# Batch 0 of an attention and feed-forward kernel by head halves, with a new order of all instructions

## The chip, the core and the metric

The kernel runs on one core of a Trainium2 chip. A core has TensorE (PE, with its weight loads listed as PEld), VectorE (DVE), ScalarE (ACT), GpSimd (POOL) and SyncE (SP), each with its own queue of instructions that it works through in order, and 16 DMA engines that move data between the chip's main memory and the core's. DMAs are issued by SP, ACT or POOL. The metric is the device time of one execution in microseconds (us), the median of three runs.

## The reference, cut to what matters

```python
# q, k, v: (8 batches, 8 heads, 576 tokens, 64), w_in: (512, 2048), w_out: (2048, 512), float32
theta = pi / 2 * arange(576) / 576
def phi(x):                                  # 64 -> 128 features
    r = maximum(x, 0)
    return concatenate([r * cos(theta), r * sin(theta)], axis=-1)
kv  = einsum('bhsf,bhsd->bhfd', phi(k), v)   # per batch and head, 128 x 64
z   = sum(phi(k), axis=tokens)
num = einsum('bhsf,bhfd->bhsd', phi(q), kv)
den = einsum('bhsf,bhf->bhs', phi(q), z) + 1e-6
x   = (num / den) as (8 * 576 tokens, 512)
h   = x @ w_in
out = (h * cos(h)) @ w_out                   # (4608, 512) float32
```

The kernel computes in 16-bit floats with 32-bit accumulation.

## The kernel before, in words

**Tiling.** Each batch has 576 tokens, treated as four tiles of 128 tokens and a rest of 64. The rests of the eight batches form a ninth chunk of 512 tokens. `raw` holds the loaded q, k, v of one batch in 32 bits (tiles `qm`, `km`, `vm`). `prep` (L336) applies the relu and the cosine or sine factor to one token tile and writes 16 bits into `KQ` (L346 on ACT, L347 on DVE). `cast_v` (L351) casts v into `V1` (L360 ACT, L361 DVE, L362 POOL), beside a column of ones that yields z. `q_pe` (L396) transposes q on PE (L402) and copies it out of PSUM (L406 ACT, L408 DVE). `kv` (L365) is the key-value product over five token tiles (L373), copied into `kvz` (L385, L387, L390). `num` (L419) multiplies q with kvz (L435) and normalises on DVE: add 1e-6 (L451), reciprocal (L453), multiply (L455). `x_pe` (L468) transposes the result on PE (L475) and ACT copies it into `xT` (L479). From batch 2 on, many of these transposes are done by DMA instead (L412, L485).

**Layers.** `layer1` for batches 0 and 1 (L513 to L538) makes 16 groups of eight matmuls of 256 columns each (L529): four quarters of w_in, two halves of the 512 tokens (two token tiles each), two groups per quarter and half. A group ends in a bank of PSUM (`M1`, three of them), from which ACT takes the cosine (L502) and DVE the product (L504) into `gT`. `layer2_plain(0)` (L773) has eight groups of eight matmuls of 512 columns (L786): four token tiles for the first half of w_out (ACT copies the result, L794), then four for the second half (DVE adds, L797). Later batches use sums of operands to save matmuls (L596 to L720, L809, L822 to L928; their matmuls are L561, L667 and L861).

**The order.** `Plan` (L138) collects steps, each with the tiles it reads and writes. The order in which all steps are emitted, and the engine of each step that can run on more than one, come from two tables written out in the file, `STARTS` (L18) and `ENGS` (L118): steps are sorted by their entry in `STARTS`. The waits follow from the tiles. Every engine then works through its own queue in that order.

**Start.** `first_attention` (L988) clears the fifth token tile of k and v, runs 28 filler matmuls on constants (`warm`, L945), and loads q, k and v of batch 0 through SP, v in two head halves of four heads each. `weights` (L948) issues w_in in four quarters from POOL, with a conversion to 16 bits on the way (L956), behind a small POOL cast that reads k (L950), and the first half of w_out (L970) behind a small copy that reads w_in's first quarter (L960). After the q transposes come 17 more filler matmuls, k and v, both halves of `kv`, and then tile by tile `num`, filler (4, 3 and 2 matmuls) and `x_pe`.

**Second batch.** `second_attention` (L1015) loads k, q, v of batch 1, v in head halves, behind four small POOL casts (`hold_raw`, L973 to L977) that read the third quarter of w_in, the last one issued. The second half of w_out is issued (L970) behind a small POOL cast that reads q of batch 1 (`part_of_w_out`, L979 to L986). PE order around it: four groups of `layer2_plain(0)` among the rest of layer 1 of batch 0 and the transposes and products of batch 1; then the group of token tile 0 with w_out's second half; then two x transposes of batch 1 and layer 1 of batch 1.

Of the kernel before, what the change touches and what calls it, by code (L numbers as in the profile page):

```python
# [16 lines left out]

STARTS = (  # L18
# [166 lines left out]
def kernel(  # L185
# [12 lines left out]
    P = 128  # L198
# [816 lines left out]
    def second_attention():  # L1015
        T = start[1] - 30
        for nm in ORDER1:
# [4 lines left out]
            if nm == ORDER1[HOLDW]:  # L1022
                part_of_w_out(nm, 1)
# [103 lines left out]
```

## Time and profile before

| what | value |
|---|---|
| time, median of 3 runs | 281.58 us (281.47 to 283.69) |
| span of the profiled execution, first to last instruction | 279.7 us |
| PE busy | 272.6 us (97%) |
| PE weight loads busy | 215.5 us (77%) |
| DVE busy | 236.9 us (85%) |
| ACT busy | 210.2 us (75%) |
| POOL busy | 82.9 us (30%) |
| clock granted to TensorE | 1.00 in all stretches |
| data moved by DMA | 58.03 MB, mean 207 GB/s |
| last matmul ends | 275.0 us |

The profile comes from one execution; its own time is given only as this span, and the median of the runs is 1.9 us above it. All times in views of the trace count from the start of the span. Busy time of PE includes the modelled ends of pipelined matmuls, so a short wait between matmuls can hide in it. In the share lines "x" is the number of instructions. In lists of groups, `out<-in` names the tiles; the arrow in brackets at the end tells how long the engine stood idle before an instruction and what ended that.

### The profile page before, as it was taken

Reading aid. Unit: us, or ns where it says so; the run is one execution under the profiler, and the core shown is the slowest. Engines: PE = TensorE matmul, PEld = TensorE weight load, DVE = VectorE, ACT = ScalarE, POOL = GpSimd, SP = SyncE. Lnnn points to the kernel's source line nnn. Section 1 sums busy time; section 2 is a strip of 40 time slices with the busy share of each in tenths; the row PEclk is TensorE's granted clock in tenths of the full one; section 3 lists DMA queues with packets and bytes.
Section 4 is the critical chain, followed back from the end, with each engine's and each line's share of the span. In section 5 each row is a group of like instructions: output and inputs, shape, how many; then the busy total and the mean of one; then the engine's idle time right before and its main releaser. Section 6 shows DMA issues by size and latency. Waiting matters only on the chain.

```text
span 279.7 us, 6825 instructions
## 1 busy us (share of the span) xinstructions
PE 272.6 (97%) x2698; PEld 215.5 (77%) x2698; DVE 236.9 (85%) x442; ACT 210.2 (75%) x363; POOL 82.9 (30%) x102
## 2 busy tenths in 40 slices
PE   8999999999999999999999999999999999999993
PEld 2567857787966677769777878789988888888882
DVE  1767698989999999999999998989989879873952
ACT  2756699879998897788989988995758686776330
POOL 1430020030501201520340045132534372399210
PEclk9999999999999999999999999999999999999999
DMA  6999989999999999989999998549756495698125
GB/s 207 312 202 206 340 239 241 361 301 174 335 261 271 258 249 246 234 268 259 255 258 246 242 229 284 98 115 141 163 75 139 110 156 105 152 143 123 75 77 150
DMA packets 80223, 58.03 MB, mean 207 GB/s; under 512 B 43200, under 2 KB 77248, under 8 KB 80192
## 3 DMA queue, kind: packets, MB, share of 16 engines
q1 hardware_dynamic: 68960, 39.99, 59.4%
q0 software_dynamic: 10496, 17.04, 30.1%
q10 hardware_dynamic: 736, 0.57, 0.7%
q8 instruction: 21, 0.34, 0.5%
q14 instruction: 10, 0.08, 0.1%
HBM read 36.75 MB, written 11.80 MB: 174 GB/s over the span
## 4 chain that ended last, share of the span: by engine, by line
PE 92%; ACT 3%; DVE 2%; issue 1%; POOL 0%; ACTq 0%; POOLq 0%
PE M L861 34%; PE M L667 14%; PE M L561 11%; PE M L529 9%; PE TR L667 6%; PE ATT L945 5%; PE ATT L435 3%; PE M L786 3%; PE ATT L373 3%; PE TR L561 2%; ACT KQ L346 2%; DVE x L455 1%; PE M L402 1%; PE M L373 0%; PE TR L475 0%
## 5 line engine op out<-in xcount | busy, mean ns | idle before, releaser
L861 PEld LDWEIGHTS <-gT 128*128 128x128 f16 x560 | 53.9, 98 | 8.3
L861 PE MATMUL M<-w_out_sb,gT 128*128 128x256 f16 x448 | 57.1, 273 | 0.0
L504 DVE TENSOR_TENSOR gT<-M,ch 128x512 f16<-128x512 f32 x73 | 48.5, 685 | 5.9 <-ACT ch L502 5.7
L502 ACT ACTIVATE ch<-M 128x512 f32<-128x512 f32 x75 | 43.4, 596 | 12.0 <-PE M L529 5.4
L346 ACT ACTIVATE KQ<-km,CS 128x512 f16<-128x512 f32 x57 | 38.5, 717 | 1.4 <-DMA km<-in_k_dram 1.3
L872 ACT ACTIVATE ost<-M 128x512 f32<-128x512 f32 x41 | 24.3, 596 | 17.9 <-PE M L861 13.0
L346 ACT ACTIVATE KQ<-qm,CS 128x512 f16<-128x512 f32 x46 | 31.5, 720 | 4.1 <-DMA qm<-in_q_dram 4.1
L561 PE MATMUL M<-xT,w_in_sb 128*128 128x512 f16 x136 | 33.8, 379 | 0.0
L861 PE MATMUL M<-T,S 128*128 128x256 f16 x256 | 32.4, 273 | 0.0
L667 PEld LDWEIGHTS <-w_in_sb 128*128 128x128 f16 x288 | 27.3, 98 | 4.8 <-issue 0.3
L362 POOL CAST V<-vm 128x1024 f16<-128x1024 f32 (+1 forms) x18 | 15.9, 907 | 50.8 <-DVE den L451 20.7
L529 PE MATMUL M<-xT,w_in_sb 128*128 128x256 f16 x256 | 30.3, 273 | 0.3 <-DVE gT L504 0.3
L861 PEld LDWEIGHTS <-S 128*128 128x128 f16 x256 | 24.8, 98 | 4.1 <-DVE S L837 0.2
L529 PEld LDWEIGHTS <-w_in_sb 128*128 128x128 f16 x256 | 24.4, 98 | 3.9 <-issue 0.5
L679 DVE TENSOR_TENSOR Z<-M,Z 128x512 f32<-128x512 f32 x31 | 21.1, 687 | 4.3 <-PE M L667 3.1
L561 PEld LDWEIGHTS <-w_in_sb 128*128 128x128 f16 x160 | 14.9, 98 | 12.2
L504 POOL TENSOR_TENSOR gT<-Z,ch 128x512 f16<-128x512 f32 x5 | 6.3, 1268 | 56.6 <-ACT ch L502 20.0
L455 DVE TENSOR_TENSOR x<-ATT,rec 128x512 f16<-128x512 f32 x32 | 22.1, 691 | 1.1
L435 PEld LDWEIGHTS <-qT 128*128 128x128 f16 (+1 forms) x320 | 14.8, 101 | 5.6 <-issue 3.5
L690 ACT ACTIVATE ch<-Z 128x1024 f32<-128x1024 f32 x12 | 12.7, 1057 | 6.9 <-DVE Z L679 4.8
L675 ACT ACTIVATE Z<-M 128x512 f32<-128x512 f32 x26 | 15.1, 596 | 3.4 <-PE M L667 2.4
L435 PE MATMUL ATT<-kvz,qT 128*128 128x65 f16 (+1 forms) x288 | 16.0, 195 | 0.8 <-DVE x L455 0.5
(150 smaller groups left out, 519.3 us busy)
## 6 DMA issues: line engine op xcount, KB each, us to landing
out_dram<-ost POOLq DMA_DIRECT2D x38, 256.0 KB, 4.3
qm<-in_q_dram SPq DMA_DIRECT2D x8, 640.0 KB, 6.7
km<-in_k_dram SPq DMA_DIRECT2D x8, 640.0 KB, 7.1
qm<-in_q_dram SPq DMA_DIRECT2D x8, 512.0 KB, 6.0
km<-in_k_dram SPq DMA_DIRECT2D x8, 512.0 KB, 6.0
vm<-in_v_dram SPq DMA_DIRECT2D x6, 640.0 KB, 5.7
vm<-in_v_dram SPq DMA_DIRECT2D x6, 512.0 KB, 4.6
w_in_sb<-in_moe_w_in_dram POOLq DMA_DIRECT2D x4, 512.0 KB, 8.8
```

The source lines that it names most:

```text
L346: fn = {"ACT": lambda: nc.scalar.activation(out=out_, in_=in_, func=AF.Relu, scale=sc), "DVE": lambda: nc.vector.tensor_scalar(out=out_, i ...
L362: "POOL": lambda: nc.gpsimd.tensor_copy(out=out_, in_=in_)}
L435: nc.tensor.matmul(bank[hb][ps, hh * D1:(hh + 1) * D1], lhsT=x[:, h, :], rhs=z[:, h, :], start=True, stop=True)
L455: nc.vector.tensor_tensor(out=split(x16[n][:, hs, :], k), in0=A[:, :, :, 0:D], in1=split(rec[n][:, hs], k).unsqueeze(3).broadcast_to((P, k ...
L502: act(0.5, due, lambda: nc.scalar.activation(out=ch[c], in_=bank, func=AF.Sin, bias=math.pi / 2.0, scale=1.0), [key], [("ch", c)])
L504: mul(due, 0.61, lambda q: q.tensor_tensor(out=dst, in0=bank if len(dst.shape) == 2 else bank.rearrange("p (j s) -> p j s", j=dst.shape[1] ...
L529: nc.tensor.matmul(M1[m][:, jj * 2 * P:(jj + 1) * 2 * P], lhsT=w_in_sb[:, cc, j * P:(j + 1) * P], rhs=X[:, cc, ts], start=(cc == 0), stop= ...
L561: nc.tensor.matmul(M, lhsT=w_in_sb[:, cc, j * P:(j + 1) * P], rhs=X[:, cc, :], start=(cc == 0), stop=(cc == NCT - 1))
L667: nc.tensor.matmul(bank[0][:, j * TH:(j + 1) * TH], lhsT=a(cc, j), rhs=b[:, cc, :], start=(first and j == 0 and cc == 0), stop=(last and j ...
L679: dve(0.61, due + 0.3, lambda: nc.vector.tensor_tensor(out=dst, in0=bank[0], in1=dst, op=ALU.add), [bank[1], key], [key])
L861: nc.tensor.matmul(bank[0][:, tt * MH:(tt + 1) * MH], lhsT=a[:, j, tt * P:(tt + 1) * P], rhs=b[:, j, :], start=(first and (apart or tt == ...
L872: act(0.5, due, lambda: nc.scalar.activation(out=dst, in_=view(bank), func=AF.Copy), [bank[1]], dk)
```

## The change: what it does

It puts batch 0 on a path of its own, `first_attention_halves`. q stays as it was (relu steps and transposes of whole tiles). k is prepared per head half (four heads, 256 columns per step), v is cast per head half with two token tiles in one instruction, and `kv_half`, `num_pair` and `x_pair` work on one head half: `num_pair` fills two banks with two token tiles and normalises both tiles of the half in one set of three DVE instructions; `x_pair` transposes both tiles into one bank and one copy takes them to `xT`. Filler is 20 matmuls at the start, 12 around the first `kv_half`, and two per `num_pair`. Layer 1 of batches 0 and 1 goes through its groups in another sequence of quarters and token halves. In batch 1, v casts also take two token tiles at once, and steps can go to either engine.

On POOL, a further small cast (through the tile `HP`) stands between q of batch 1 and the cast that releases w_out's second half. The new code can also split w_in, with its second half behind the v casts (`WS2`), but this option is `None` here: the four quarters are issued together behind k, in the same order as before. `RAW1=2` and `WO2=1` name the same w_in quarter and the same tensor q as before. `STARTS` and `ENGS` are new for the whole program (1376 steps for 1363). Options not shown here (`F16`, `MODE`, `H1`, `DA`, `SQ`, `L2F` and others) are off and leave the steps as they were.

```diff
+OPT = dict(WS2=None, W2F=2, HH='kv', LD=[['q', 3], ['k', 3], ['v', 0], ['v', 1]], XB=[['B3'], ['B3', 'M1']],
+           W0=5, W1=6, WF=[[2, 2], [2, 2]], HOLD=['k', 0], P0=1, RAW1=2, WO2=1, ...)
...
-    den = [sb(f"den{n}", [P, H], F32) for n in range(NX)]
-    rec = [sb(f"rec{n}", [P, H], F32) for n in range(NX)]
-    x16 = [sb(f"x16_{n}", [P, H, D]) for n in range(NX)]
+    DEN, REC = [sb(n, [P, NX, H], F32) for n in ("den", "rec")]
+    den, rec = [[x[:, n] for n in range(NX)] for x in (DEN, REC)]
+    XN = sb("XN", [P, NX, H, D])
+    x16 = [XN[:, n] for n in range(NX)]
...
-            for quarter in range(4):
-                for hf in range(2):
+            for quarter, hf in ([(q_ + i, hf) for q_ in (0, 2) for hf in range(2) for i in range(2)] if OPT["HH"] else
+                                [(q_, hf) for q_ in range(4) for hf in range(2)]):
...
     def part_of_w_out(nm, n):
...
+        if OPT["W2F"]:
+            src, rd = raw[nm][0:2, 0, 0, 0:1], [((nm, 0), 0)]
+            for i in range(OPT["W2F"] - 1):
+                pl.add("POOL", 0.2, 0.3, 0, lambda i=i, src=src: nc.gpsimd.tensor_copy(
+                    out=HP[:, 2 + i:3 + i], in_=src), rd, [("hop", 2 + i)])
+                src, rd = HP[:, 2 + i:3 + i], [("hop", 2 + i)]
+            pl.add("POOL", 0.2, 0.3, 0, lambda src=src: nc.gpsimd.tensor_copy(
+                out=w_out_sb[0:2, n * JH:(n + 1) * JH, 0].rearrange("p (g j) -> p g j", g=2)[:, :, 0],
+                in_=src.broadcast_to((2, 2))), rd, [("w_out", g) for g in (2 * n, 2 * n + 1)])
+        else:
+            pl.add("POOL", 0.2, 0.3, 0, hold, hk(nm, [0], [0]), [("w_out", g) for g in (2 * n, 2 * n + 1)])
         w_out_load(2 * n, 2 * n + 2)
...
+    def kv_half(hb, bank, key, due, b=0):
+        hs = range(H)[HALVES[hb]]
...
+                for t in range(NT + 1):
+                    nc.tensor.matmul(
+                        bank[:, hh * D1:(hh + 1) * D1], lhsT=kp[:, t, h].rearrange("p g d -> p (g d)"),
+                        rhs=V1[:, t, h, :], start=(t == 0), stop=(t == NT))
...
+        copy_by_either(Z[:, hb], bank[:, 0:HB * D1], due, 0.4, 0.38, [key], [("kvz", b, hb)])
...
+    def num_pair(i, hb, due, b=0):
+        hs = HALVES[hb]
+        for t in (2 * i, 2 * i + 1):
+            bank, key = ATT[:, t % 2, :], ("ATT", t % 2)
...
+                for hh in range(HB):
+                    nc.tensor.matmul(bank[:, hh * D1:(hh + 1) * D1], lhsT=qT[t][:, hb * HB + hh, :],
+                                     rhs=kvz[b][:, hb * HB + hh, :], start=True, stop=True)
...
+        def norm():
+            nc.vector.tensor_scalar_add(out=denp[:, n], in0=A[:, :, :, D], scalar1=1e-6)
+            nc.vector.reciprocal(out=recp[:, n], in_=denp[:, n])
+            nc.vector.tensor_tensor(out=XF[:, hb, 2 * i:2 * i + 2], in0=A[:, :, :, 0:D],
+                                    in1=recp[:, n].unsqueeze(3).broadcast_to((P, 2, HB, D)), op=ALU.mult)
...
+    def half_tiles(hb, due):
...
+        for nm in OPT["HH"]:
+            if nm == "k":
+                for t in range(NT + 1):
+                    for g in range(2):
+                        prep(0, "k", t, g, "", due, hs)
+            elif nm == "v":
+                for t, nt in ((0, 2), (2, 2), (4, 1)):
+                    cast_v(0, t, ("DVE", "ACT", "POOL"), due, hs, nt=nt)
+                kv_half(hb, *BANKS2[hb], due)
...
+        if hb == 0:
+            for i in range(OPT["W1"]):
+                warm(2, 0.4314, ATT[:, 1, :], [("TR", 0)] if i == 0 else [], [("ATT", 1)])
+        if OPT["P0"]:
+            for i in range(NT // 2):
+                num_pair(i, hb, due + 2 * i)
+                n = OPT["WF"][hb][i]
+                if n:
+                    warm(n, 0.2157 * n, M1[1], [("ATT", 1)], [("M1", 1)])
+                x_pair(i, hb, *pick[kb_[i % len(kb_)]], due + 2 * i)
...
+    def first_attention_halves():
+        for i, nm in enumerate("kv"):
+            dve(0.53, i - 9, lambda nm=nm: nc.vector.memset(raw[nm][:, :, NT, :], 0.0), [],
+                hk(nm, ts=[NT]))
+        for i in range(OPT["W0"]):
+            warm(4, 1.293)
+        for nm, x in OPT["LD"]:
+            load(0, nm, 0, HALVES if x == 2 else (slice(0, H),) if x == 3 else (HALVES[x],))
...
+        for hb in range(2):
+            half_tiles(hb, 4 + 4 * hb)
...
-    first_attention()
+    (first_attention_halves if OPT["HH"] else first_attention)()
     layer1(0)
     second_attention()
```

More of the change, by code (lines that the diff above doesn't have):

```diff
@@ L282 @@
     ORDER0, ORDER1, HOLDW, W_FIRST = "qkv", "kqv", 1, None
-    GATE1 = (w_in_sb[0:2, 0, Dff // 2 + 1:Dff // 2 + 2], [("w_in", 2)])
+    R1 = OPT["RAW1"]
+    GATE1 = ((w_in_sb[0:2, 0, R1 * Dff // 4 + 1:R1 * Dff // 4 + 2], [("w_in", R1)]) if R1 < 4 else
+             (w_out_sb[0:2, (R1 - 4) * NJT // 4, 1:2], [("w_out", R1 - 4)]))
+    HOLDW, W_FIRST = OPT["WO2"], OPT["WFI"]
     src = {"k": k, "v": v, "q": q}
@@ L344, in prep @@
         f = len(heads) / H
-        cost = {"DVE": 0.09 + 0.33 * f, "ACT": 0.12 + 0.5 * f}
+        cost = {"DVE": 0.09 + FD * f, "ACT": 0.12 + 0.5 * f}
         fn = {"ACT": lambda: nc.scalar.activation(out=out_, in_=in_, func=AF.Relu, scale=sc),
@@ L362, in cast_v @@
               "POOL": lambda: nc.gpsimd.tensor_copy(out=out_, in_=in_)}
-        either(due, {e: cost[e] for e in ([eng] if eng else VCAST)}, fn, rd, wr)
+        either(due, {e: cost[e] for e in ([eng] if isinstance(eng, str) else eng)}, fn, rd, wr)
+    full = {}
     def kv(b, due, pair=None):
@@ L398, in q_pe @@
         ps = bank.bitcast(F16).rearrange("p (h s) -> p h s", h=H)
+        more = [("qTh", t % NT, hb) for hb in range(2)] if b <= 1 and OPT["HH"] else []
         def mm():
@@ L458, in norm, with norm2 @@
                     op=ALU.mult)
-        dve(1.05 if pair is None else 1.15, due, norm, keys, [("x16", n)])
+        if OPT["DA"] and pair is None and b >= 2:
+            A, (hs, k, ks) = N[0], cut[0]
+            act(0.22, due, lambda: nc.scalar.activation(
+                out=split(den[n][:, hs], k), in_=A[:, :, :, D], func=AF.Identity, bias=EPS, scale=1.0),
+                keys, [("den", n)])
+            def norm2():
+                nc.vector.reciprocal(out=rec[n], in_=den[n])
+                nc.vector.tensor_tensor(
+                    out=split(x16[n][:, hs, :], k), in0=A[:, :, :, 0:D],
+                    in1=split(rec[n][:, hs], k).unsqueeze(3).broadcast_to((P, k, HB, D)), op=ALU.mult)
+            dve(0.87, due, norm2, keys + [("den", n)], [("x16", n)])
+            return n
+        dve(1.05 if pair is None else 1.15, due, norm, keys, [("x16", n)]
+            + ([("x16h", n, hb) for hb in range(2)] if b == 1 and OPT["HH"] else []))
         return n
@@ L476, in mm @@
                                  is_transpose=True)
+        full[key] = False
         pe(NCT, MMT, due, mm, [("x16", n), "ID", *after], [key])
@@ L577 @@
     LATE = min(c for c, nf in FAST1.items() if nf > 2)
-    assert all(FAST1[c] == NJT // 4 for c in range(LATE, NC))
     def flat(t, dt=F16):
@@ L946, in warm @@
         pl.add("PE", us, us, -1, go, rd, wr)
+        pl.steps[-1]["ni"] = n
     def weights():
@@ L1013, in first_attention, with both, copy_by_either @@
             x_pe(0, t, t, *BANKS[3 - t % 2], "ACT", 8 + t, [("fill", t)])
+    def both(due, cost, fn, rd, wr, lat={"DVE": 0.13, "ACT": 0.15}):
+        pl.add([(e, cost[e], cost[e] + lat[e], fn[e]) for e in cost], 0, 0, due, None, rd, wr)
+    def copy_by_either(out_, in_, due, dc, ac, rd, wr):
+        both(due, {"DVE": dc, "ACT": ac}, {
+            "DVE": lambda: nc.vector.tensor_copy(out=out_, in_=in_),
+            "ACT": lambda: nc.scalar.activation(out=out_, in_=in_, func=AF.Copy)}, rd, wr)
@@ new lines, in q_half, with mm @@
+    def q_half(t, hb, bank, key, due):
+        hs = HALVES[hb]
+        ps = bank.bitcast(F16)[:, 0:HB * P].rearrange("p (h s) -> p h s", h=HB)
+        full[key] = False
+        def mm():
+            for hh in range(HB):
+                nc.tensor.matmul(ps[:, hh, :], lhsT=qp[:, t, hb * HB + hh].rearrange("p g d -> p (g d)"),
+                                 rhs=IDENT, is_transpose=True)
+        pe(HB, MMT, due, mm, [("qp", t, g, h) for g in range(2) for h in range(H)[hs]] + ["ID"], [key])
+        copy_by_either(qT[t][:, hs, :], ps, due, 0.4, 0.5, [key], [("qTh", t, hb)])
@@ new lines, in num_half, with mm @@
+    def num_half(t, hb, bank, key, due, b=0):
+        n = t if b == 0 else xcount[0] % NX
+        full[key] = False
+        hs = HALVES[hb]
+        def mm():
+            for hh in range(HB):
+                nc.tensor.matmul(bank[:, hh * D1:(hh + 1) * D1], lhsT=qT[t][:, hb * HB + hh, :],
+                                 rhs=kvz[b][:, hb * HB + hh, :], start=True, stop=True)
+        pe(HB, MMA, due, mm, [("qTh", t, hb) if b == 0 else ("qT", t), ("kvz", b, hb)], [key])
+        A = bank[:, 0:HB * D1].rearrange("p (h d) -> p h d", h=HB)
+        def norm():
+            nc.vector.tensor_scalar_add(out=den[n][:, hs], in0=A[:, :, D], scalar1=1e-6)
+            nc.vector.reciprocal(out=rec[n][:, hs], in_=den[n][:, hs])
+            nc.vector.tensor_tensor(out=x16[n][:, hs, :], in0=A[:, :, 0:D],
+                                    in1=rec[n][:, hs].unsqueeze(2).broadcast_to((P, HB, D)), op=ALU.mult)
+        dve(0.76, due, norm, [key], [("x16h", n, hb)])
@@ new lines, in x_half, with mm @@
+    def x_half(t, hb, bank, key, due, after=(), b=0, n=None):
+        n = t if b == 0 else n
+        full[key] = False
+        cs = slice(hb * NCT // 2, (hb + 1) * NCT // 2)
+        ps = bank.bitcast(F16)[:, 0:NCT // 2 * P].rearrange("p (c s) -> p c s", c=NCT // 2)
+        x2 = x16[n].rearrange("p h d -> p (h d)")
+        def mm():
+            for i, c in enumerate(range(NCT)[cs]):
+                nc.tensor.matmul(ps[:, i, :], lhsT=x2[:, c * P:(c + 1) * P], rhs=IDENT, is_transpose=True)
+        pe(NCT // 2, MMT, due, mm, [("x16h", n, hb), "ID", *after], [key])
+        copy_by_either(xT[b][:, cs, t * P:(t + 1) * P], ps, due, 0.28, 0.36, [key] + ([("xTh", b, t)] if hb else []),
+                       [("xT", b, t) if hb else ("xTh", b, t)])
@@ new lines, in x_pair, with mm @@
+    def x_pair(i, hb, bank, key, due, b=0):
+        full[key] = False
+        cs = slice(hb * NCT // 2, (hb + 1) * NCT // 2)
+        ps = bank.bitcast(F16)[:, 0:NCT * P].rearrange("p (c s) -> p c s", c=NCT // 2)
+        def mm():
+            for j in range(2):
+                x2 = XF[:, hb, 2 * i + j].rearrange("p h d -> p (h d)")
+                for c in range(NCT // 2):
+                    nc.tensor.matmul(ps[:, c, j * P:(j + 1) * P], lhsT=x2[:, c * P:(c + 1) * P], rhs=IDENT,
+                                     is_transpose=True)
+        pe(NCT, MMT, due, mm, [("XF", b, i, hb), "ID"] + [("x16", n) for n in range(NX)], [key])
+        ts = [2 * i, 2 * i + 1]
+        copy_by_either(xT[b][:, cs, 2 * i * P:(2 * i + 2) * P], ps, due, 0.42, 0.5,
+                       [key] + ([("xTh", b, t) for t in ts] if hb else []),
+                       [("xT", b, t) if hb else ("xTh", b, t) for t in ts])
@@ L1029, in second_attention @@
             for g in range(2):
-                prep(1, "q", t, g, "DVE" if g == 0 else "ACT", due)
+                prep(1, "q", t, g, E1 or ("DVE" if g == 0 else "ACT"), due)
             if t < NT:
@@ L1033, in second_attention @@
         for hb in range(2):
+            if OPT["HH"]:
+                for t, nt in ((0, 2), (2, 2), (4, 1)):
+                    cast_v(1, t, ("DVE", "ACT", "POOL"), T + 4 + hb, HALVES[hb], nt=nt)
+                continue
             for t in range(NT + 1):
                 cast_v(1, t, "ACT" if t % 2 else "DVE", T + 4 + hb, HALVES[hb])
+        if OPT["H1"]:
+            for hb in range(2):
+                kv_half(hb, ATT[:, hb, :], ("ATT", hb), T + 6, 1)
+            if OPT["H1"] == 2:
+                for i in range(NT // 2):
+                    for hb in range(2):
+                        num_pair(i, hb, T + 8 + 2 * i, 1)
+                        x_pair(i, hb, *(BANKS[3], BANKS[2])[hb], T + 8 + 2 * i, 1)
+            for hb in range(2 if OPT["H1"] == 1 else 0):
+                for t in range(NT):
+                    num_half(t, hb, ATT[:, t % 2, :], ("ATT", t % 2), T + 8 + t, 1)
+                    x_half(t, hb, *(BANKS[3], BANKS[2])[t % 2], T + 8 + t, (), 1, xcount[0] % NX)
+                    xcount[0] += 1
+            q_pe(1, NT, *BANKS[3], "ACT", start[1] + 10)
+            n = num(1, NT, start[1] + 12)
+            x_pe(1, NT, n, *BANKS[3], "ACT", start[1] + 12)
+            return
         kv(1, T + 6)
```

267 lines of the change are left out of this document (207 added, 60 removed), and 197 rows, old and new, of the table STARTS.

## The prediction

> **What bounds the kernel now.** I read the page's share line first: PE 97%, and the windows view adds that the clock granted to TensorE is 1.00 in every stretch. So the end moves only with PE's stalls and with the time at which its dense work begins. The chain of work, cut to the first 25 us, shows that beginning (start, length, engine, tile, line):
>
> ```profile
> 1.32 9.04 PE ATT L945 x28
> ...
> 11.25 3.67 PE ATT L945 x17
> ...
> 15.37 1.22 PE M L373 x40
> ...
> 16.62 0.44 DVE kvz L387
> ...
> 18.16 0.76 DVE x L455 x2
> ...
> 22.48 0.76 DVE x L455 x2
> 23.23 0.61 DVE gT L504
> ...
> 23.88 10.72 PE M L529 x96
> ```
>
> L945 is filler on constants. The first real chain is L373 (key-value product), kvz, four normalisations on DVE (17.67 to 23.23), then layer 1 of batch 0 (L529), of which 16 of its 128 matmuls are already done at 23.88.
>
> The windows view (us, busy time and instructions of PE, weight loads, DVE, ACT, POOL, then clock, DMA share, GB/s) tells what is left after that:
>
> ```profile
> 34.40:50.27 15.87, 15.62 (x179) 10.48 (x178) 14.96 (x41) 13.97 (x26) 1.85 (x3) 1.00 1.01 255
> 50.27:275.00 224.73, 224.71 (x2239) 183.25 (x2236) 200.53 (x351) 176.73 (x305) 74.28 (x81) 1.00 0.88 198
> ```
>
> At 50.27 layer 1 of batch 1 starts. Behind it lie, by the page's groups, 1528 matmuls of 256 columns at 0.109 us (0.87 for eight in the chain), 184 of 512 at 0.216, 240 of L373 at 0.0305, 192 of L435 at 0.0335 and 64 half ones at 0.028, 28 transposes at 0.056: 166.9 + 39.8 + 7.3 + 8.2 + 1.6 = 223.8 us. They take 224.7. A new order can win at most **0.9 us** there.
>
> The third view is the timeline around the hand-over, with the DMA view's times from issue to landing:
>
> ```profile
> 38.01 0.19 POOL L982 CAST w_out_sb<-qm 2x2 f16<-2x2 f32 x1 [11.79 <-DMA qm<-in_q_dram]
> 38.49 1.66 POOL L970 DMA_DIRECT2D w_out_sb<-in_moe_w_out_dram  x2 [0.30 <-POOL w_out_sb L982]
> ...
> 48.09 1.89 PE L786 MATMUL M<-w_out_sb,gT 128*128 128x512 f16 x8
> 49.82 0.61 PE L475 MATMUL M<-IDENT,x 128*128 128x128 f16 x8
> ```
>
> POOL waits 11.79 us for q of batch 1, then issues w_out's second half. Alone, its first DMA has 5.6 us to landing; both together a median of 7.5, so the second 9.4: issued near 39.24, landed near 48.64. L786 comes in groups of eight matmuls; the group of 48.09, the fifth, is the first to use this half: its matmul 5, at 48.09 + 4 x 0.216 = 48.95, reads what the second DMA brings. **The slack is 0.3 us.**
>
> **The change, part by part.** 1. *Batch 0 by head halves.* Loads and their order are unchanged, so q lands at 7.2, k at 10.5, the v halves at 12.2 and 13.7 (issues at 4.33 and 5.66, 7.8 and 8.0 to landing). I walk the new order with rows of before: 512-column relu steps 0.41 on DVE and 0.65 on ACT; 256-column ones, not in the trace, between the DVE cast of that size (0.28) and half of 0.41, taken as 0.27, on ACT 0.40 like its cast; pair casts of 512 columns as 0.45. Filler: 14 slow matmuls at 0.43 and 6 at 0.216 end at 8.6. The four q transposes end at 10.3. k's and v's first half: DVE 7 x 0.27 + 0.45 + 0.28 from 10.5, 13.2; ACT 13.3. First kv half 13.9; its copy behind q's third ACT copy (1.02 from 13.3), 14.7. Four DVE norms of 1.09 (0.17 + 0.20 + 0.69 and gaps): the first from 15.1, behind second-half k and v steps; the second from 16.6, the third from 18.15 behind a 0.42 copy, the fourth from 20.0 behind another. Layer 1 starts at 20.2, pauses for the last transpose at 21.4 and is dense with 8 of its matmuls done. Before had 16 done at 23.88; the changed one has them at 22.25. Part 1 wins **1.65 us**. The filler saved (54 to 40) is in this. If 256-column steps cost 0.35, DVE is 1 us later and the win 0.7.
>
> 2. *Split of w_in.* The code is there but its option is off: all four quarters still go out behind k, and the last lands at about 25.5 (POOL's gate at 25.67). 0.
>
> 3. *Batch 1's gates and loads.* POOL's four small casts now run q, v, v, k; SP's k load is first in SP's queue and waits for the last one, 0.37 us later (26.04 against 25.67). The DMA engines are full from 14 to 38, so the landings move by 0 to 0.37; I take 0.3 for q, which lands last of its two DMAs at 37.8.
>
> 4. *w_out's second half.* It waited for q before, too. Its cast still waits for both q DMAs (it reads partitions 0 and 1, one from each block), and one more cast stands ahead of it: 0.48 us, the distance of cast and issue above. First issue 38.49 + 0.3 + 0.48 = 39.27, second 40.0; with 9.4 to landing, **49.4**. Batch 2's loads leave within 0.3 us of before (42.2), those of q earlier (45.3 for 47.3), so nothing makes the landing shorter; I take 9.5 and 49.5.
>
> 5. *The second attention.* Walked the same way from k at 35.0, q at 38.1, v at 40 and 41: PE is at the fifth L786 group at 47.3, 0.8 ahead of before and no longer 1.65, because kv (42.4) and its copy (44.0) hang on landings. Matmul 5 of the group would run at 48.15 and waits to 49.5: an added stall of 1.35. Queued behind it on PE: two x transposes and all of layer 1 of batch 1. 49.5 + 4 x 0.216 + 0.45 = 50.8 for 50.27: **+0.5**. So part 1's win is hidden by a transfer that the change makes later. Bounds: -0.8 if w_out is no limit (47.3 + 1.73 + 0.45 = 49.5), +1.5 if it lands at 50.5.
>
> 6. *The rest of the table.* Counts by kind and engine are the same within one relu step. One place differs to the eye: near 75 us the last tile of batch 2 goes num, then x transposes of the tile before, then its own x transposes, with no layer 1 group between as before had (75.35, 0.87). PE waits there for a norm: 1.09 + 0.04 less 0.22 = **+0.9**. Elsewhere 0, bounds -0.9 (above) and +3 (stalls as dense as now, 0.9, made fourfold by thinner margins: DVE is busy 200.5 of 224.7 us).
>
> **Sum**: -1.65 + 0.85 (lost to landings up to 47.3) + 1.35 (wait inside the fifth L786 group) = +0.5 with the rounding of the walk, + 0.9 = +1.4 us. On the profiled span, 279.7 becomes 281.1; the median of the runs is 281.58, 1.9 above that span (start and end lie around it), and I carry the difference over: **283.0**. A measurement of this kernel can tell about 1%, 2.8 us, from no change.
>
> **Rivals.** *A: w_out is in time.* If the landing stays below 48.2, layer 1 of batch 1 starts at 49.5 and the 0.9 is made good or not: -0.8 to +0.1, near 281.0. For it: PE showed no wait at 48.95. Against: the added cast. *B: the early win goes through.* -1.65 and up to -0.9: 279.0 to 280. It needs landings before 47 and an earlier v; the 16 DMA engines' share of 1.01 to 1.25 speaks against. *C, slower: the clock.* In 12.4 to 20.2 us PE is busy 7.23 of 7.80 before; in the change, two kv halves 1.2, filler 2.2, nums 1.1 and transposes 0.7 make 5.2 of 7.8. If the clock falls, it must be won back: at the start that took 1.32 to 7.2, 14 matmuls at 0.43 for 0.216, 3.0 us lost. PE then reaches the fifth group at 50.3 and layer 1 of batch 1 at 52.5: +2.2 + 0.9, 284.7. It decides once the busy share falls under what kept 1.00; the lowest such row is 2.90 of 3.40 (17.9 to 21.3). The Trainium skill, "TensorE: Matmul & The Clock Gate" (What's actually happening), drops the clock only after an idle window of about 3.4 us; by it C would cost 0, as no pause of the walk exceeds 1.5. *D, slower: w_out starts later still.* Between its issue and 41.0 the DMA moved 47 GB/s (39.5 to 41) while DVE was busy 1.50 of 1.50. In the change the v casts, 0.45 + 0.28 + 0.45, fall on that start; if they hold it up, +1.2: 284.2. The Trainium skill, "SBUF — State Buffer" (SBUF: two separate sides), says just this: a copy in VectorE's two-port mode locks GpSimd out of writing the descriptors of its DMAs. *E, slower:* the new order stalls throughout, +3 in part 6 for +0.9: 285.
>
> **Chances.** Forecast 0.45 (282 to 284), A 0.20, B 0.07, C 0.06, D 0.10, E 0.12. To leave out no more than 2 in 10 the range takes in A and most of E: 280.0 to 285.6. Faster by over 1% (below 278.8): 0.05. Slower by over 1% (above 284.4): E, most of C, half of D: 0.23. Within: 0.72.
>
> **What would show it.** Layer 1 of batch 0 dense from 21 to 22; w_out's second issue at 40.0; a pause of PE inside the first L786 of w_out's second half until about 49.5; layer 1 of batch 1 at 50.8; a pause of 0.9 near 77; the clock at 1.00. I am wrong if that L786 runs through, or if layer 1 of batch 1 starts below 49.5 or after 52.

## The result and the profile after

The changed kernel takes **283.13 us**, the median of 11 runs (281.87 to 285.98); the kernel before, run beside it, takes 282.11. The ratio is **1.0047, with a 95% interval of 1.0026 to 1.0068**: about 1.3 us slower (1.0 us by the two medians), more than the spread of these runs explains and still within the 1% that the prediction took as no change. The span of the profiled execution is 281.5 us for 279.7, so 1.8 us longer.

The windows view of the changed kernel (us, busy time and instructions of PE, weight loads, DVE, ACT, POOL, then clock, DMA share, GB/s) puts both losses in their places:

```profile
12.40:20.20 7.80, 5.52 (x87) 3.50 (x87) 6.82 (x20) 4.52 (x10) 3.51 (x6) 1.00 1.16 196
...
35.25:51.06 15.81, 13.97 (x170) 9.70 (x169) 13.88 (x38) 12.00 (x22) 2.25 (x4) 1.00 0.96 243
51.06:276.79 225.73, 224.72 (x2239) 183.32 (x2236) 199.73 (x351) 176.32 (x303) 74.14 (x81) 1.00 0.90 197
```

Layer 1 of batch 1 starts at 51.06 (before: 50.27), 0.79 us later. Behind it PE is busy for 224.72 us as it was before (224.71), but over 225.73 us in place of 224.73: one more idle microsecond. 0.79 + 1.00 is the whole 1.8 us. In the first row PE is busy only 5.52 of 7.80 us, and the clock stays at 1.00.

The chain of work of the changed kernel up to its dense layer 1 (start, length, engine, tile, line), the counterpart of the first view of the kernel before:

```profile
1.31 6.75 PE ATT L1033 x20
...
10.46 1.62 DVE KQ L364 x6
...
12.85 0.75 DVE V L378 x2
...
13.77 1.09 DVE KQ L364 x3
...
19.17 0.70 DVE XN L1233
...
21.19 0.70 DVE XN L1233
...
21.94 0.40 PE M L1246 x4
22.34 2.63 PE M L570 x24
```

From k's landing at 10.4 to 15.5 the chain runs over DVE's relu steps and casts alone. Layer 1 of batch 0 is dense from 22.17 with 8 matmuls done, so 16 are done at 22.17 + 0.87 = 23.04; before had 16 done at 23.88. The early win is **0.84 us**.

The same chain around the hand-over to batch 1:

```profile
27.78 10.29 DMA qm<-in_q_dram
...
38.22 0.19 POOL HP L1103
...
38.46 0.40 POOL w_out_sb L1106
...
39.15 0.74 POOL w_out_sb L1085
39.89 9.82 DMA w_out_sb<-in_moe_w_out_dram
...
49.75 1.02 PE M L872 x4
```

It leaves PE at 25 us and comes back at 49.75: load of q, the added cast through `HP`, the cast that releases w_out, its second issue at 39.89, 9.82 us to landing. In the kernel before, no load stands in the chain between 24 and 56 us. Finally PE's own timeline at the two places, with the idle time ahead of an instruction and what ended it in brackets:

```profile
47.09 1.03 PE L872 MATMUL M<-w_out_sb,gT 128*128 128x512 f16 x4
...
49.75 1.02 PE L872 MATMUL M<-w_out_sb,gT 128*128 128x512 f16 x4 [1.63 <-DMA w_out_sb<-in_moe_w_out_dram]
...
51.06 1.91 PE L570 MATMUL M<-xT,w_in_sb 128*128 128x256 f16 x16
...
78.93 0.40 PE L514 MATMUL TR<-IDENT,XN 128*128 128x128 f16 x4 [1.00 <-DVE XN L480]
```

The fifth group of L872 is cut in two: four matmuls at 47.09, then 1.63 us of waiting for w_out, then the other four. These are the only waits of PE over 0.25 us behind 20 us. The idle time in brackets counts from the modelled end of the matmul before; by the pace of 0.216 us per matmul the group stands still from 47.95 to 49.75, 1.80 us.

### The profile page after: what moved, and what is told of

Same layout as the page of the kernel before. It is cut to its first block, busy times and chain, and to the rows that moved or that the text cites. A ratio compares the mean times of both kernels' runs of the same rounds, so it can differ in the third digit from the quotient of the medians.

```text
span 281.5 us, 6806 instructions
## 1 busy us (share of the span) xinstructions
PE 270.2 (96%) x2684; PEld 213.9 (76%) x2684; DVE 239.0 (85%) x445; ACT 208.2 (74%) x358; POOL 82.9 (29%) x103
## 4 chain that ended last, share of the span: by engine, by line
PE 85%; DMA 7%; DVE 4%; POOL 1%; issue 1%; SPq 0%; ACT 0%; POOLq 0%; DVEq 0%
PE M L947 34%; PE M L731 14%; PE M L603 11%; PE M L570 6%; PE TR L731 6%; DMA qm<-in_q_dram 4%; DMA w_out_sb<-in_moe_w_out_dram 3%; PE ATT L459 3%; PE ATT L392 3%; PE ATT L1033 2%; PE M L872 2%; PE TR L603 2%; DVE KQ L364 1%; DVE XN L1233 1%; PE M L423 1%
## 5 line engine op out<-in xcount | busy, mean ns | idle before, releaser
L947 PEld LDWEIGHTS <-gT 128*128 128x128 f16 x560 | 53.9, 98 | 7.5
L947 PE MATMUL M<-w_out_sb,gT 128*128 128x256 f16 x448 | 56.9, 273 | 0.0
L363 ACT ACTIVATE KQ<-km,CS 128x512 f16<-128x512 f32 (+1 forms) x58 | 37.6, 686 | 1.3 <-DMA km<-in_k_dram 1.3
L603 PE MATMUL M<-xT,w_in_sb 128*128 128x512 f16 x136 | 33.7, 379 | 0.0
L363 ACT ACTIVATE KQ<-qm,CS 128x512 f16<-128x512 f32 x44 | 30.1, 717 | 4.3 <-DMA qm<-in_q_dram 4.3
L947 PE MATMUL M<-T,S 128*128 128x256 f16 x256 | 32.4, 273 | 0.0
L570 PE MATMUL M<-xT,w_in_sb 128*128 128x256 f16 x256 | 29.6, 273 | 0.0
L947 PEld LDWEIGHTS <-S 128*128 128x128 f16 x256 | 25.0, 98 | 4.8
L603 PEld LDWEIGHTS <-w_in_sb 128*128 128x128 f16 x160 | 14.8, 98 | 12.1
L480 DVE TENSOR_TENSOR XN<-ATT,rec 128x512 f16<-128x512 f32 x30 | 20.7, 691 | 1.0
L739 ACT ACTIVATE Z<-M 128x512 f32<-128x512 f32 x26 | 15.1, 596 | 4.2 <-PE M L731 3.4
L364 DVE TENSOR_SCALAR KQ<-qm,CS 128x512 f16<-128x512 f32 x28 | 12.4, 478 | 5.2 <-DMA qm<-in_q_dram 5.2
L872 PE MATMUL M<-w_out_sb,gT 128*128 128x512 f16 x64 | 15.1, 379 | 1.6 <-DMA w_out_sb<-in_moe_w_out_dram 1.6
```

The lines of the kernel that those rows point to most:

```text
L363: fn = {"ACT": lambda: nc.scalar.activation(out=out_, in_=in_, func=AF.Relu, scale=sc), "DVE": lambda: nc.vector.tensor_scalar(out=out_, i ...
L480: nc.vector.tensor_tensor(out=split(x16[n][:, hs, :], k), in0=A[:, :, :, 0:D], in1=split(rec[n][:, hs], k).unsqueeze(3).broadcast_to((P, k ...
L570: nc.tensor.matmul(M1[m][:, jj * 2 * P:(jj + 1) * 2 * P], lhsT=w_in_sb[:, cc, j * P:(j + 1) * P], rhs=X[:, cc, ts], start=(cc == 0), stop= ...
L603: nc.tensor.matmul(M, lhsT=w_in_sb[:, cc, j * P:(j + 1) * P], rhs=X[:, cc, :], start=(cc == 0), stop=(cc == NCT - 1))
L872: nc.tensor.matmul(M, lhsT=G[:, j, t * P:(t + 1) * P], rhs=w_out_sb[:, j, :], start=(j == jh * JH), stop=(j == (jh + 1) * JH - 1))
L947: nc.tensor.matmul(bank[0][:, tt * MH:(tt + 1) * MH], lhsT=a[:, j, tt * P:(tt + 1) * P], rhs=b[:, j, :], start=(first and (apart or tt == ...
```

## The experiments

My theory: the change loses in two places. Up to layer 1 of batch 1 it loses 0.79 us by w_out's landing: PE comes to the fifth group 1.00 us earlier than before, but waits there, so that the 0.84 us won at the start are hidden. Then it loses 1.00 us by the order of one tile. The first arrival of q of batch 0, with the same loads in all kernels, is seen at 7.16 to 8.15 us in the thirteen profiles, and in the variants of the changed kernel nearly all of PE's work moves along with it up to the fifth group. w_out's landing does not. a_gap and a_gap2 below have the changed kernel's order up to 75 us, so their wait in that group is the same experiment again (PE's timeline, a_gap first):

```profile
48.02 1.03 PE L872 MATMUL M<-w_out_sb,gT 128*128 128x512 f16 x4
49.46 1.02 PE L872 MATMUL M<-w_out_sb,gT 128*128 128x512 f16 x4 [0.41 <-DMA w_out_sb<-in_moe_w_out_dram]
```

```profile
47.28 1.03 PE L872 MATMUL M<-w_out_sb,gT 128*128 128x512 f16 x4
49.38 1.02 PE L872 MATMUL M<-w_out_sb,gT 128*128 128x512 f16 x4 [1.08 <-DMA w_out_sb<-in_moe_w_out_dram]
```

With q at 8.09, 7.34 and 7.16 (a_gap, a_gap2, the change) PE waits 0.41, 1.08 and 1.63 us, and layer 1 of batch 1 starts at 50.76, 50.69 and 51.06: the start is set by the landing, not by when PE arrives, and the wait of 1.63 us is the longest of the three. So a time of one profile is compared with another's only with this arrival beside it (7.16 in the changed kernel, 7.23 in the one before), and the ratios come from the timed runs. They are all against the kernel before, in the same set of runs.

| run | built on | edit | ratio and 95% interval |
|---|---|---|---|
| the change | | | 1.0047 (1.0026 to 1.0068) |
| a_nohop | changed | no further POOL cast | 1.0012 (0.9999 to 1.0026) |
| a_group | changed | fifth L872 group later | 1.0034 (1.0022 to 1.0047) |
| a_gap | changed | last tile of batch 2 reordered | 1.0015 (1.0002 to 1.0029) |
| a_late | changed | 1.08 us of filler ahead of layer 1 | 1.0041 (1.0025 to 1.0057) |
| b_hop | before | with the further POOL cast | 1.0024 (1.0006 to 1.0042) |
| a_krel | changed | w_out released by k | 0.9996 (0.9985 to 1.0007) |
| a_gap2 | changed | a_gap, and two copies of ACT earlier | 1.0025 (1.0006 to 1.0045) |
| a_nohop_gap2 | changed | a_nohop and a_gap2 | 1.0049 (1.0031 to 1.0067) |
| a_krel_gap2 | changed | a_krel and a_gap2 | **0.9977 (0.9964 to 0.9991)** |
| a_krel_late | changed | a_krel and the filler | 1.0022 (1.0012 to 1.0031) |
| b_krel | before | w_out released by k | 0.9995 (0.9980 to 1.0010) |

**a_nohop: one cast less on POOL.**

```diff
-W2F=2
+W2F=1
+STARTS, ENGS = STARTS[:153] + STARTS[154:], ENGS[:153] + ENGS[154:]
```

> The changed kernel without the extra small POOL cast; the cast that releases w_out's second half reads q itself, as before the change. Theory (the wait of 1.63 us inside the fifth L872 group hangs on w_out's landing, and the landing on its issue): both w_out DMAs are issued 0.45 to 0.55 us earlier (first at 38.65 for 39.15), the second half of that group starts at 49.2 to 49.3 for 49.75, layer 1 of batch 1 at 50.5 to 50.6 for 51.06, and the span falls by 0.45 to 0.55 (281.0 for 281.5; about 1.003 of the kernel before). Rival (the landing is set by the DMA engines' load, not by the issue): the group starts at 49.6 to 49.8 and nothing changes. Rival (PE waits there for something else too): the wait shrinks but layer 1 of batch 1 stays at 51.0.

w_out's first issue is at 38.41 for 39.15, with q of batch 0 0.25 later. PE's timeline:

```profile
48.80 1.02 PE L872 MATMUL M<-w_out_sb,gT 128*128 128x512 f16 x4 [0.43 <-DMA w_out_sb<-in_moe_w_out_dram]
```

The wait falls from 1.63 to 0.43 us, layer 1 of batch 1 starts at 50.11, and the median is 282.48. The landing follows the issue, and 50.11 lies ahead of all three starts above. The profile moves by more than the cast's 0.5 us because q of batch 1 also landed earlier in it (its POOL cast at 37.61 for 38.22). Against the medians of before beside each (282.09 and 282.11), the medians differ by 0.63 us, near the 0.5 us of the cast.

**a_group: the waiting group later in PE's order.**

```diff
+STARTS[235], STARTS[236], STARTS[213] = 4941, 5113, 4768
```

> The changed kernel with other places in the order for three steps and nothing else: the fifth L872 group stands behind both x transposes and the first two layer-1 groups of batch 1 on PE, one of the x transposes between these two groups, and its DVE add behind their two products. Theory (PE loses 1.63 us only because the group stands ahead of work that could run): PE now waits about 0.7 us for the norm of token tile 3 (ends 47.77), then runs; the group starts at 50.0 to 50.2, after w_out landed at 49.7, without a wait; sum of waits there 0.7 for 1.63, span 0.8 to 1.0 lower (280.5 to 280.7). Rival (DVE and ACT carry no more there): PE stalls on products or banks between 50 and 54 and the gain is below 0.3. Rival (w_out's landing moves with the order): no gain.

The time hardly falls. PE's timeline shows how the win is lost again:

```profile
47.76 0.62 PE L514 MATMUL M<-IDENT,XN 128*128 128x128 f16 x4 [0.24 <-DVE XN L480]
...
58.82 1.02 PE L872 MATMUL M<-w_out_sb,gT 128*128 128x512 f16 x4 [0.20 <-DVE ost L883]
...
134.90 0.30 PE L459 MATMUL ATT<-kvz,qT 128*128 128x65 f16 x4 [0.62 <-DMA qT<-KQ]
```

The group itself starts at 50.23 without a wait. Against the same matmuls of the changed kernel, PE is 0.85 us ahead at 55.5 (1.1 with the later q counted), 0.34 ahead at 60.9, and from 136 us to the end 0.3 behind. Where DVE is busy for 5.93 of the 6.00 us from 55 to 61, 0.5 us are lost again, and the wait of 0.62 us for a transpose of q by DMA takes the rest. The expectation held for the first 8 us only. The second loss has no link to the edit that the trace would show; it stays open whether it is one of the moved order or of that execution.

**a_gap and a_gap2: the pause near 78.** On PE, num and the x transposes of that tile go ahead of one L947 group; on DVE its normalisation goes ahead of one product. a_gap2 also moves two copies on ACT ahead (the second line of the diff).

```diff
+STARTS[349], STARTS[348], STARTS[350], STARTS[346] = 7290, 7295, 7300, 7301
+STARTS[347], STARTS[352], STARTS[452] = 7360, 7535, 7536
```

> The changed kernel with other places in the order for the last tile of batch 2 alone: its num, normalisation and the x transposes of the tile before go ahead of one L947 group (1.04 us), and on DVE the normalisation ahead of one product. Theory (the pause of 1.00 us at 78.93 is the normalisation with no PE work beside it): the L947 group covers it, pause 0.0 to 0.2, span 0.8 to 1.0 lower (280.5 to 280.7). Rival (the pause moves: the product that is now later, or a later group, is waited for instead): the pause is gone, a new one of 0.3 or more stands within 10 us behind it and the gain is below 0.6.

> The changed kernel with the last tile of batch 2 ordered as in the run named a_gap, and on ACT two copies of transposed tiles moved ahead: one in front of a copy of layer 2's result, one in front of a relu step of batch 3's q. Theory (what stayed in that run, 0.53 us, was ACT's copy that frees the one bank of the transposes): the pause of 1.00 us near 78 falls to 0.1 to 0.3, the first L603 group comes 0.7 to 0.9 us earlier against layer 1 of batch 1, and the time is 0.7 to 0.9 us under the changed kernel's. Rival (the relu step that is now later makes a transpose by DMA late): the pause goes and a wait on qT of 0.3 or more appears between 85 and 140.

PE's timeline of a_gap, then of a_gap2:

```profile
78.16 0.38 PE L514 MATMUL TR<-IDENT,XN 128*128 128x128 f16 x4 [0.53 <-ACT xT L519]
```

```profile
77.78 0.40 PE L514 MATMUL TR<-IDENT,XN 128*128 128x128 f16 x4 [0.18 <-DVE XN L480]
```

The pause was the normalisation with no PE work beside it, as I had read it, and behind it stood a second limit, ACT's copy out of the one bank of these transposes. Measured from the start of layer 1 of batch 1, the first L603 group comes 0.5 us earlier in a_gap and 0.8 in a_gap2 (0.6 from 84 us on). In the medians this is 0.3 and 0.75 us against those of before beside them (282.09, 282.19; the change lies 1.02 above its own); a_gap2's ratio, spread over 281.54 to 284.57, does not show it as clearly.

**a_late: is the early win hidden?** Five more filler matmuls stand ahead of layer 1 of batch 0.

```diff
-WF=[[2, 2], [2, 2]]
+WF=[[2, 2], [2, 7]]
```

> The changed kernel with five more filler matmuls of 512 columns (1.08 us of PE) just ahead of layer 1 of batch 0; nothing is left out. Theory (the early win of about 0.85 us of batch 0's new path is hidden by landings, w_out's last): layer 1 of batch 0 begins 0.9 to 1.1 later, the wait inside the fifth L872 group falls from 1.63 to 0.5 to 1.0, layer 1 of batch 1 still begins at 51.0 to 51.2, and the span changes by 0 to 0.2. Rival (batch 0's start carries through to the end): layer 1 of batch 1 begins 0.9 to 1.1 later and the span is 282.4 to 282.6.

Layer 1 of batch 0 is dense 1.24 us later than in the changed kernel, 0.41 of it from q; so the filler itself delays it by 0.83 us, as much as the early win, and the rest of its 1.08 us fills the pause of PE ahead of batch 0's last x transposes. PE's timeline, and ACT's further on:

```profile
49.70 1.02 PE L872 MATMUL M<-w_out_sb,gT 128*128 128x512 f16 x4 [0.33 <-DMA w_out_sb<-in_moe_w_out_dram]
...
82.37 2.75 PE L603 MATMUL M<-xT,w_in_sb 128*128 128x512 f16 x12 [0.95 <-ACT xT L519]
```

```profile
81.12 0.72 ACT L363 ACTIVATE KQ<-qm,CS 128x512 f16<-128x512 f32 x1 [1.67 <-DMA qm<-in_q_dram]
```

Layer 1 of batch 1 starts at 51.00 for 51.06, and the ratio (1.0041 for 1.0047) does not move: work of the size of the early win, added at the start, is free, so the early win is hidden. The profiled execution is the slowest of this kernel's, 285.34 us, and shows two waits that the changed kernel's profile hasn't: 0.61 us for a transpose of q by DMA (78.16), and 0.95 us because ACT stands in a relu step that waits for q of batch 3, ahead of the copy that PE needs. Two of the changed kernel's 11 runs took 285.6 and 286.0, none of the kernel before's took over 283.8. That these two lost their time in the same place is likely, but not shown.

**b_hop: the added cast alone, in the kernel before.**

```diff
-    WARM = sb("WARM", [P, 1], F32)
+    HP, WARM = sb("HP", [2, 4]), sb("WARM", [P, 1], F32)
...
+            nc.gpsimd.tensor_copy(out=HP[:, 2:3], in_=raw[nm][0:2, 0, 0, 0:1])
...
-                in_=raw[nm][0:2, 0, 0, 0:1].broadcast_to((2, 2)))
+                in_=HP[:, 2:3].broadcast_to((2, 2)))
```

> The kernel before the change, with nothing new but the further small POOL cast between q of batch 1 and the cast that releases w_out's second half. In the four profiles of the changed kernel's variants that wait for w_out, 10.1 to 10.6 us pass from its first issue to the matmul that uses its last quarter. Theory (before had next to no slack there, so the cast alone makes PE wait): first issue at 38.9 to 39.1 for 38.49, landing at 49.1 to 49.6, a wait of 0.2 to 0.6 us inside the fifth L786 group (before: none), layer 1 of batch 1 at 50.4 to 50.9 for 50.27, time 1.0005 to 1.002 of the kernel before. Rival (before had slack of over half a microsecond, and only the change's earlier PE exposes the landing): no wait, 50.27, ratio 1.000.

The chain of work of b_hop:

```profile
40.24 10.29 DMA w_out_sb<-in_moe_w_out_dram
...
50.58 1.02 PE M L786 x4
```

PE waits 0.99 us, more than the 0.2 to 0.6 expected, and layer 1 of batch 1 starts at 51.88 (before: 50.27; 0.45 of it from q of batch 0): the landing took 10.29 us from the second issue, where the six profiles of the changed kernel and its variants whose chain goes through it have 9.31 to 9.82. The time rises by 0.24%, about 0.7 us. So the cast alone costs about half as much as the whole change (0.47%), though the interval reaches from 0.06% to 0.42%, and before had next to no slack.

**a_krel, b_krel: w_out released by k.**

```diff
-                part_of_w_out(nm, 1)
+                part_of_w_out("k", 1)
```

> The changed kernel with the release of w_out's second half reading k of batch 1 (landed at 34.9 to 35.2) in place of q (38.2); all else as in the changed kernel. Theory A (the wait hangs on the late issue): issue at 35.7 to 36.0, landing before 47, no wait inside the fifth L872 group, layer 1 of batch 1 at 49.4 to 49.6 for 51.06, span 1.2 to 1.6 lower (279.9 to 280.3). Theory B (the DMA engines are full until 38, so w_out's 2.1 MB push batch 1's q and v back by 1 to 2.5 us): q lands at 39 to 40, v at 42 to 43, the key-value product ends 1 to 2 us later than 43.1, layer 1 of batch 1 at 50.5 to 51.5, span within 0.6 of 281.5.

> The kernel before the change with w_out's second half released by k of batch 1 in place of q, and nothing else. Theory (before had no wait for w_out, so there is nothing to win): w_out issued near 36, layer 1 of batch 1 at 50.0 to 50.4 for 50.27 against the same arrival of q of batch 0, ratio 0.999 to 1.000. Rival (w_out in front of v on the DMA engines holds up v): key-value product of batch 1 later than 42.25 by 0.3 or more, ratio 1.001 or more. Rival (in many executions before does wait for w_out, with the first q a little later): ratio 0.997 to 0.999.

In a_krel w_out is issued at 36.60, and the fifth group runs through. Its PE timeline and its chain of work, then the windows view of the changed kernel and of a_krel over the same stretch:

```profile
47.55 1.89 PE L872 MATMUL M<-w_out_sb,gT 128*128 128x512 f16 x8
...
49.72 1.91 PE L570 MATMUL M<-xT,w_in_sb 128*128 128x256 f16 x16
```

```profile
33.74 8.26 DMA vm<-in_v_dram
...
42.78 0.77 PE ATT L392 x20
```

```profile
38.00:42.00 4.00, 4.00 (x51) 2.62 (x49) 3.44 (x9) 3.70 (x8) 2.25 (x4) 1.00 0.57 128
```

```profile
38.00:42.00 4.00, 4.00 (x45) 2.52 (x43) 3.90 (x8) 3.52 (x7) 0.27 (x1) 1.00 1.18 257
```

Between 38 and 42 the DMA engines of the changed kernel had a hole (share 0.57, 128 GB/s); with the release by k it is filled (1.18, 257). The key-value product's second part is only 0.2 us later against q's arrival. Theory A holds, and with it the loss is gone (0.9996). In this profile the limit is now v's landing at 42.00. The early release is not free: in the four profiles that have it, the last load of v takes 8.26 to 8.99 us from issue to landing, in the other nine 7.90 to 8.17. In the kernel before the same edit wins nothing (0.9995); the chain of b_krel runs over the slowest of these loads:

```profile
33.74 8.99 DMA vm<-in_v_dram
```

**a_krel_late: does the early win count once w_out is out of the way?**

> The changed kernel with w_out's second half released by k of batch 1, and five more filler matmuls (1.08 us of PE) ahead of layer 1 of batch 0; nothing is left out. In a_late, where w_out was released by q, the same filler left the start of layer 1 of batch 1 where it was. Theory (w_out's landing alone hid the early win): with it gone the filler costs its length less the 0.46 us that PE waited for v in a_krel: layer 1 of batch 1 0.5 to 0.7 us later than in a_krel, time 0.0015 to 0.0025 above a_krel's ratio. Rival (v's landing hides the rest as well): 0 to 0.2 us later, ratio within 0.0008 of a_krel's.

Layer 1 of batch 1 starts at 50.73, 1.01 us later than in a_krel, of which q's arrival (7.79 for 7.37) is 0.42: the filler costs 0.6 us there. Of its 1.08 us, 0.25 fill the pause ahead of batch 0's last x transposes, as in a_late, and 0.25 go into PE's wait for v (0.46 us in a_krel, 0.21 here). The ratio is 0.0026 above a_krel's, some 0.7 us, just over the 0.0015 to 0.0025 expected. So w_out's landing hid the early win, and with w_out released earlier most of it counts.

**The mends together.**

> Both mends together: without the further POOL cast, and with the last tile of batch 2 ordered as in a_gap2. Theory (the two waits of 1.63 and 1.00 us make up the changed kernel's whole loss, and they are independent): layer 1 of batch 1 at 50.0 to 50.5, no pause over 0.3 near 78, PE 0.1 to 0.4 us ahead of the kernel before from 80 on, time 0.997 to 1.000 of the kernel before. Rival (other waits take their place further on, as one of 0.6 us on a transpose by DMA did at 134.9 when the fifth L872 group was moved): time 1.001 or more.

> The changed kernel with both mends that worked alone: w_out's second half released by k of batch 1, and the last tile of batch 2 ordered as in a_gap2. Theory (the two waits are independent): no wait inside the fifth L872 group, at most 0.3 us near 77, time 0.996 to 0.998 of the kernel before, 0.2 to 0.35% under a_krel. Rival (num of that tile now runs a L947 group earlier and waits there for the transpose of q by DMA, which needs about 7 us from its issue near 69 to 71, as in a_nohop_gap2): a wait on qT of 0.3 to 1.1 us near 77, time 0.999 to 1.002.

PE's timeline of a_nohop_gap2, then of a_krel_gap2:

```profile
77.70 0.43 PE L459 MATMUL ATT<-kvz,qT 128*128 128x65 f16 x8 [1.10 <-DMA qT<-KQ]
```

```profile
76.47 0.43 PE L459 MATMUL ATT<-kvz,qT 128*128 128x65 f16 x8 [0.77 <-DMA qT<-KQ]
```

a_krel_gap2 is faster than both kernels: 281.57 us (281.33 to 282.76), 0.23% under the kernel before, though its profile, taken in the slowest of its executions, shows num waiting for q's transpose. a_nohop_gap2 is no faster than the change itself, although both of its edits won something alone; in its profile the same wait, 1.10 us, has taken the pause's place, beside 0.69 us for w_out (q of batch 0 arrived at 8.15). Its six runs are all at 282.58 or above. With a_gap2's order num asks for that transpose at about 76 us in place of 77.3: in a_gap2 it landed at 76.0, just in time, in a_krel_gap2 at 76.4 and in a_nohop_gap2 at 77.7, too late. Why it lands later there, and whether that is what makes these six runs slow, stays open.

## Why the prediction was right

283.0 was predicted for 283.13, with no change as the likeliest. That the two agree to 0.1 us is partly luck: the forecast was +1.4 us on a kernel before at 281.58, and the runs show +1.0 (medians) to +1.3 (ratio) on one at 282.11. The mechanism, a win at the start that w_out's later landing hides and a pause near 78, is the one that the runs show. Several of its terms were off, and some of the errors cancelled.

1. *Batch 0.* Forecast: 1.65 us won, layer 1 at 20.2, dense at 21.4. Measured: 0.84, 20.84 and 22.17. **The first mis-sized term** is the 256-column relu step on DVE, taken as 0.27. The groups of the changed kernel from 10 to 21 us, shapes kept apart, give 4.1 us for 12:

```profile
L364 DVE TENSOR_SCALAR KQ<-km,CS 128x256 f16<-128x256 f32 x12 | 4.1, 398 | 0.1
```

That is 0.34, which the prediction kept as its other case (0.35, win 0.7). Seven such steps ahead of the first key-value half cost 0.5 us more than I had counted. They did not delay its copy, which ends at 14.71 as forecast (14.7). But DVE comes later to the first normalisation, 15.45 for 15.1, and that is about half of the loss. The other half grows between the normalisations, as DVE's and PE's timelines show:

```profile
15.45 0.15 DVE L1231 TENSOR_SCALAR den<-ATT 128x8 f32<-128x8 f32 x1
...
16.63 0.41 PE L1224 MATMUL ATT<-kvz,qT 128*128 128x65 f16 x8 [1.01 <-DVE XN L1233]
...
17.08 0.17 DVE L1231 TENSOR_SCALAR den<-ATT 128x8 f32<-128x8 f32 x1 [0.24 <-PE ATT L1224]
...
18.73 0.17 DVE L1231 TENSOR_SCALAR den<-ATT 128x8 f32<-128x8 f32 x1 [0.19 <-PE ATT L1224]
...
20.76 0.15 DVE L1231 TENSOR_SCALAR den<-ATT 128x8 f32<-128x8 f32 x1
```

num waits for the normalisation ahead of it, and the next normalisation for num. The three distances are 1.63, 1.65 and 2.03 us, where the walk had 1.5, 1.55 and 1.85. So the fourth starts at 20.76 for 20.0. No run varies the relu step alone; this division is read from the trace.

2. *Split of w_in:* off, as said. POOL's first gate behind w_in ran at 24.89 all the same, 0.78 us earlier than before, where the old 25.67 was forecast.

3. and 4. *Gates and w_out's release.* Forecast: first issue 39.27, second 40.0, matmul 5 waiting to 49.5. Measured: 39.15, 39.89, 49.75. The numbers held, the reason given for one of them did not. The new order of the gates was to hold up the load of k by 0.37 us. The gates ran earlier in place of later, and the load of k was issued at 25.46 for 25.88 before:

```profile
25.46 0.60 SPq L338 DMA_DIRECT2D km<-in_k_dram  x1
```

POOL's cast behind q still ran at 38.22 for 38.01, 0.21 us later, near the 0.3 taken. So the earlier issue bought nothing at the landing; what held q up no run settles. The 9.5 us from w_out's second issue to landing were 9.82. The slack of 0.3 us in before was no more than that: b_hop waited 0.99.

5. *Second attention.* Forecast: PE at the fifth group at 47.3, wait 1.35, layer 1 of batch 1 at 50.8. Measured: 47.09, 1.63, 51.06. By PE's pace, as the forecast counts it, the wait was 1.80 for 1.35. I had the early win lose 0.85 of 1.65 to landings on the way to 47.3. In the trace the 0.84 us came through whole, and 0.16 more was won on the way (47.09 for 48.09). So two errors cancelled, which was luck, and the hidden part was right: a_late shows that work added at the start is free, and a_krel_late that most of it isn't once w_out is early.

6. *The table.* Forecast: 0.9 us near 77, 0 elsewhere. Measured: 1.00 at 78.93, and no other. The layer 1 group that the kernel before has in that place starts at 74.13, not at 75.35 as I wrote. My sum for the profile was +1.4; +1.8 came, 0.26 of the rest from layer 1 of batch 1 (51.06 for 50.8) and 0.1 from the pause.

*The rivals.* A (w_out in time) and B (the early win goes through) fell: the group waited. C fell: the clock was 1.00 in every stretch up to the last matmul, with PE busy 5.52 of 7.80 us in the window where I had worked out 5.2. The clock column alone would not settle it, since it reads 1.00 in the first 5 us too, where filler takes 0.43 us each. The lengths do: from 5.96 on filler takes 0.216, and layer 1 takes 0.109 (24 in 2.63). The Trainium skill, "TensorE: Matmul & The Clock Gate" (What's actually happening), has the clock fall only after an idle window of about 3.4 us; no pause between matmuls was longer than 1.8, and that far the trace agrees. Behind the last matmul, which ends at 276.79, it does not: the windows view has the clock at half from 279.0, after 2.2 us of an idle PE.

```profile
276.79:278.99 2.20, 0.00 (x1) 0.00 (x0) 0.46 (x2) 0.00 (x0) 0.00 (x0) 1.00 0.89 275
279.01:281.50 2.49, 0.00 (x0) 0.00 (x0) 0.00 (x0) 0.00 (x0) 0.00 (x0) 0.50 0.23 73
```

So the wait of 1.8 us stood nearer to such a fall than 3.4 us suggests. D (VectorE's casts hold up w_out's descriptors) asked for 1.2 us more to landing: 9.82 us against the 9.5 that I took leaves 0.3 at most, and five variants with the same casts have 9.31 to 9.66. Whether the rule of the Trainium skill, "SBUF — State Buffer" (SBUF: two separate sides), stands behind those 0.3 no run here shows. E (stalls throughout) fell in this profile, but a_late's and the two runs near 286 show that such stalls are close.

## What to carry to other kernels

A win ahead of a load that is released by another load is worth nothing until the release moves: follow the chain through the DMA's issue, not only through the engine that waits. A release that is tied to the last of several loads may leave a hole on the DMA engines behind it; here an earlier one made the last load of v slower by 0.1 to 1.1 us, the key-value product 0.2 us later, and gave back all that had been lost. And a pause in a hand-ordered program is filled by work from ahead of it only if what then starts earlier has its own inputs by that time.

## What the runs showed of the hardware

- Halving a relu step from 512 to 256 columns took DVE from 0.41 us (five in 2.07 in the kernel before) to 0.34 (twelve in 4.1 in the changed one), not to half.
- The same first loads let the first relu step start between 7.16 and 8.15 us in thirteen profiles. A difference of under 1 us between two profiles needs this taken out first.
- Filler matmuls of 512 columns took 0.43 us each at the start and 0.216 from some point on. In the thirteen profiles that point lies between 4.0 and 7.2 us (5.96 in the changed kernel, 7.17 in the one before), with the same filler ahead of it.
- SP spent between 1.2 and 3.6 us on issuing one transpose by DMA between 60 and 80 us, and what stood behind it in its queue waited: in a_krel_gap2 the last one of q, ready in `KQ` at 65.1, was issued at 69.95.
